# Spectral mixing and gated FFN: batch 0's first-stage results stored in thirds, and pieces moved in pairs

## The chip, the cores and the metric

One core of a Trainium2 chip runs one program. The metric is device time in microseconds (us); before the change it was 1681.91 us, the median of 3 runs (1680.63 to 1682.58). In the code `nc.tensor` is PE, `nc.vector` DVE, `nc.scalar` ACT, `nc.gpsimd` POOL, and `nc.sync` SP, the queue that issues every DMA of this kernel.

## The reference

```python
x: (8, 3136, 256)                     # w_in, conv_w, w_out are float64 on input
X = np.fft.rfft(x, axis=1)
Yr = Xr @ w_r - Xi @ w_i + b_r        # Yi likewise, with b_i
Y  = soft_threshold(Yr, 0.01), soft_threshold(Yi, 0.01)
y  = np.fft.irfft(Y, n=3136, axis=1)
h  = np.maximum(y @ w_in, 0)          # 256 -> 1024
c  = three-tap convolution of h along the sequence, per channel
out = (h * sigmoid(c)) @ w_out        # 1024 -> 256
```

Each batch goes through a transform along the sequence, a complex matrix product with bias and threshold, the inverse transform, and then a feed-forward layer with a gate. Nothing couples the batches.

## The kernel before, in words

The sequence of 3136 is 49 times 64. Each transform is done in two stages of matrix products, with tables made on the host.

**First stage (quads, L313).** A batch's x is cut into NX = 8 pieces. A piece holds 4 of 32 columns j for both halves h: 48 of the 49 rows n of half 0 on partitions 0 to 47, those of half 1 on 64 to 111, each partition with 4 KB that are contiguous in DRAM; row 48 goes to partitions 48 and 112 by a small DMA of its own. Eight passes of PE fill two PSUM banks; ACT (L330) and DVE (L331) copy one bank each into tile `a1`; `store_a1` writes 2 x 192 KB (and 8 KB of row 48) to DRAM scratch `sc1[b]`, in which unit g of the batch is 8 consecutive rows.

**Units.** A batch has NG = 6 units; two further ones hold the zero frequency of four batches each, so there are 50 iterations `it`. Iteration `it` runs, in PE's order: stage 3 of unit it-4 (L415), one or two pieces of a later batch (`quads`, by the table `count`), stage 2 of unit `it` (L359), and the complex product of unit it-1 (`mix`, L387, 36 matmuls). Stage 2 reads tile `a2`, 512 KB loaded from `sc1[b]` (`load_a2`, L346), which spreads (position, part) over 128 partitions. Because the first stage yields its rows the other way round, a unit's load needs the stores of all eight pieces of its batch: `ask_a2` issues it only when all of them are stored in program order, and on SP the load then waits until they have landed. `a2` has 3 buffers. Behind stage 2, ACT, DVE and POOL split values in two (`fh`, `fl`; the third pair by `third`, L370 on ACT and L371 on POOL), threshold (`shrink`, L403 to L405), and add the bias (`v`, L390). Stage 3's result goes to scratch `sc2` (L430).

**Head.** Batch 0 has no earlier batch to hide behind. Its x goes to tile `hx`, its results to `ha`; the loop at L485 copies a piece, stores it and asks for a further piece of x. NW = 9 times four passes on no new data (`ps_idle`) follow on PE. Then come the mixing weights (L214), the loads of units 0 and 1, one piece of batch 1's x, row 48's store (L499) and the bias, spread over 128 partitions by the DMA itself (L227). The pools `wkf`, `wk`, `cab`, `io` then take over the memory of `hx` and `ha`.

**Order and waits.** The whole front is in an order written by hand (`manual_schedule`). SP issues its DMAs one by one; as built they take eight completion semaphores in turn, so an issue waits for the landing of the DMA eight places ahead of it: at most eight are under way, whatever their size. Tables `t2` (second stage; POOL makes their lower half, L208) and `i1` (third stage) come in small loads during the first iterations. `fetch` keeps up to XRB = 4 pieces of x loaded; `a1` has 4 buffers.

**Last stages.** From about 472 us on, the feed-forward layer runs for all batches (L602, L630), fed by the last transform stage (L156).

Of the kernel before, what the change touches and what calls it, by code (L numbers as in the profile page):

```python
# [9 lines left out]
F32 = mybir.dt.float32  # L10
# [7 lines left out]
B, S, D, FF = 8, 3136, 256, 1024  # L18
R = 49
C = 64  # L20
U = (R - 1) // 2
# [4 lines left out]
UG = 4  # L26
# [83 lines left out]
def spectral_ffn_kernel(ctx: ExitStack, tc: tile.TileContext, x, w_r, w_i, b_r, b_i,  # L110
# [6 lines left out]
    sc1 = [dram.tile([RU, C, D], F32, name=f"sc1_{b}") for b in range(B)]  # L117
# [53 lines left out]
    with ExitStack() as ab:  # L171
# [13 lines left out]
        sgn = c0.tile([P, 2, C], F32, name="sgn")  # L185
        t2 = c1.tile([K2, U + 1, K2], F32, name="t2")
        bias = cmx.tile([P, 2, D], F32, name="bias")
        cmx.tile([P, 96], F32, name="pad")
# [10 lines left out]
            nc.sync.dma_start(f1, fwd1)  # L199

        def load_t2(g):
            sl = slice(g * UG, min((g + 1) * UG, U + 1))
            nc.sync.dma_start(t2[0:C, sl, :], fwd2v[:, sl, :])

        def fill_t2(g):
# [16 lines left out]
                split(wmix_hi[:, :, k, :], wmix_lo[:, :, k, :], w)  # L222

        def load_bias():

            for k in range(2):
                nc.sync.dma_start(bias[:, k, :], (b_r, b_i)[k].partition_broadcast(P))  # L227

        def load_inv1(g):
            if g < NG:  # L230
                sl = slice(g * UG // 2, (g + 1) * UG // 2)
# [72 lines left out]
        def load_x(pool, b, jc, **kw):  # L304

            xr = pool.tile([P, JC, D], F32, name="xr", **kw)
            xv = x[b].rearrange("(n h j) d -> h n j d", h=2, j=H)[:, :, jc * JC:(jc + 1) * JC, :]
            for h in range(2):
                nc.sync.dma_start(xr[SP * h:SP * h + RU], xv[h, 0:RU])
            nc.sync.dma_start(xr[RU:P:SP], xv[:, RU])  # L310
            return xr

        def quads(ps, xr):  # L313
# [3 lines left out]
                    rows = slice(SP * h, SP * h + R)  # L317
                    nc.tensor.matmul(ps[h][SP * r:SP * (r + 1)], f1[rows], xr[rows, 2 * r:2 * r + 2, :], start=True, stop=True)  # L318

        def store_a1(b, jc, a1, all_rows=True):  # L320
            dst = sc1[b].rearrange("m (c r j) d -> r c m (j d)", r=2, j=4)
            for r in range(2):
                nc.sync.dma_start(dst[r, jc], a1[SP * r:SP * r + RU].rearrange("p j h d -> p (j h d)"))  # L323
            if not all_rows:
                return
            dst = sc0[b // BH][b % BH].rearrange("(c r j) d -> c r (j d)", r=2, j=4)
            nc.sync.dma_start(dst[jc], a1[RU:P:SP].rearrange("p j h d -> p (j h d)"))

        def copy_a1(a1, ps):
            nc.scalar.copy(a1[:, :, 0], ps[0])  # L330
# [4 lines left out]
            quads(ps, xr)  # L335
            return ps

        def stage1_out(b, jc, ps):
            a1 = s1p.tile([P, 2, 2, D], F32, name="a1", bufs=4)
            copy_a1(a1, ps)  # L340
            store_a1(b, jc, a1)

        def load_a2(b, g):
            a2 = a2p.tile([K2, UG, D], F32, name="a2")
            if g < NG:
                nc.sync.dma_start(a2, sc1[b].rearrange("(u c) j d -> (c j) u d", c=2)[:, g * UG:(g + 1) * UG, :])  # L346
# [87 lines left out]

        nc.vector.memset(mlam, -LAM)
        nc.vector.memset(warm, 0.0)
        for q in range(4):
            nc.vector.memset(sgc[32 * q:32 * (q + 1)], -1.0 if q % 2 else 1.0)
        for c in range(2):
# [8 lines left out]
        xs, vs, ss, a2s, xq = {}, {}, {}, {}, []  # L448
        p1 = nx = NX

        def fetch(n):
            nonlocal nx
            while len(xq) < n and nx < n_pc:
                xq.append(load_x(s1p, *divmod(nx, NX), bufs=XRB))
                nx += 1

        def ask_a2(*its):
            for i in its:
# [5 lines left out]
        ab.enter_context(tc.manual_schedule())  # L464
        load_f1()
        with tc.tile_pool(name="hx", bufs=1, reuse_waits="tile") as hx, tc.tile_pool(name="ha", bufs=1, reuse_waits="tile") as ha:
            xh = hx.tile([P, H, D], F32, name="hx")
            ah = ha.tile([P, NX, 2, 2, D], F32, name="ha")
            xv = x[0].rearrange("(n h j) d -> h n j d", h=2, j=H)
            hr = sc0[0][0].rearrange("(c r j) d -> r c (j d)", r=2, j=4)  # L470
            asked = 0

            def ask_x():
                nonlocal asked
                if asked < NX:
                    if asked % 2 == 0:
                        sl = slice(asked * JC, (asked + 2) * JC)
                        nc.sync.dma_start(xh[RU:P:SP, sl], xv[:, RU, sl])
                    sl = slice(asked * JC, (asked + 1) * JC)
                    for h in range(2):  # L480
                        nc.sync.dma_start(xh[SP * h:SP * h + RU, sl], xv[h, 0:RU, sl])
                    asked += 1
            for _ in range(5):
                ask_x()
            for jc in range(NX):  # L485
                copy_a1(ah[:, jc], stage1_pe(xh[:, jc * JC:(jc + 1) * JC]))
                store_a1(0, jc, ah[:, jc], False)
                ask_x()
                if jc in (4, 5):
                    load_t2(jc - 4)  # L490
                    fill_t2(jc - 4)
            idle = [psx.tile([P, 2, D], F32, name="ps_idle", tag="bank") for _ in range(2)]
            for _ in range(NW):
                quads(idle, xh[:, (NX - 1) * JC:])
# [29 lines left out]

        for it in range(n_it + LAG):
            drain = it >= n_it
            fetch(XRB)
            if 1 < it + 2 < NG:
# [4 lines left out]
            if 0 <= it - 2 < NG:  # L533
# [10 lines left out]
            ps1 = [stage1_pe(xq.pop(0)) for _ in range(n_s1)] if it > 1 else []  # L544
            if it >= LAG:
                stage3_out(*g3, ps3)
            if WP0 <= it < Y0:
                next(background, None)
            elif it == WP0 - 2:
                next(background)  # L550
            for ps in ps1:
                stage1_out(*divmod(p1, NX), ps)
                p1 += 1
            ask_a2(it + 1)
            if WP0 <= it < Y0:
                for _ in range(2):
                    next(background, None)
            if it < n_it:
                xs[it] = stage2(items[it][1], a2s.pop(it))
            if it == Y0:  # L560
                eb.close()
                zio, y_a = pool("zio", 3, side="right"), pool("y_a", side="right")
                y0 = new_y(y_a)
                z2s = []
                for _ in range(3):
                    ask_z2()
            if it == n_it - 1:
                xs[it] = third(xs[it])
            if 0 <= it - 2 < n_it:
                ss[it - 2] = (clip if drain else shrink)(vs.pop(it - 2))  # L570
            if it < n_it - 1:
                xs[it] = third(xs[it])
            if Y0 < it < Y1:
                last_stage()
            if it == 1:
                stage1_out(*divmod(p1, NX), stage1_pe(xq.pop(0)))
                p1 += 1
# [113 lines left out]
```

## Time and profile before

| what | value |
|---|---|
| median of 3 runs | 1681.91 us |
| the profiled execution | 1683.23 us, of which its span 1681.5 us |
| PE busy | 1659.8 us (99%) |
| DVE, ACT busy | 1390.0 us, 1175.9 us |
| chain that ended last, by engine | PE 95%, DMA 3% |
| DMA | 162.50 MB, mean 97 GB/s; 235 to 282 GB/s in the first nine of 40 slices (to 378 us) |

The profile is one execution. The chain that ended last is followed back from the end: at each step to what released it. A row of the timeline has start, duration, engine, line, operation, tiles written and read, count, and in brackets the idle time before it with its releaser; a row named SPq is the issue of a DMA, not its transfer. A row of the waits has engine and line, what was waited for, the total, how many times, and the longest. A row of the windows has a stretch, and for each engine its busy time in it; its last three figures are PE's granted clock, the mean busy share of the 16 DMA engines, and the rate in GB/s.

### The profile page before, as it was taken

Reading aid. Unit: us, or ns where it says so; the run is one execution under the profiler, and the core shown is the slowest. Engines: PE = TensorE matmul, PEld = TensorE weight load, DVE = VectorE, ACT = ScalarE, POOL = GpSimd, SP = SyncE. Lnnn points to the kernel's source line nnn. Section 1 sums busy time; section 2 is a strip of 40 time slices with the busy share of each in tenths; the row PEclk is TensorE's granted clock in tenths of the full one; section 3 lists DMA queues with packets and bytes.
Section 4 is the critical chain, followed back from the end, with each engine's and each line's share of the span. In section 5 each row is a group of like instructions: output and inputs, shape, how many; then the busy total and the mean of one; then the engine's idle time right before and its main releaser. Section 6 shows DMA issues by size and latency. Waiting matters only on the chain.

```text
span 1681.5 us, 30439 instructions
## 1 busy us (share of the span) xinstructions
PE 1659.8 (99%) x12400; PEld 1539.7 (92%) x12400; DVE 1390.0 (83%) x1727; ACT 1175.9 (70%) x1584; POOL 192.3 (11%) x114
## 2 busy tenths in 40 slices
PE   7999999999999999999999999999999999999998
PEld 4778888889989999999999999999999999999998
DVE  2668988877688888888888888888888888888887
ACT  2667777777677777677777776777777776776776
POOL 1534444444300000000000000000000000000000
PEclk8999999999999999999999999999999999999999
DMA  8889999886421101111111001111101111100001
GB/s 240 241 282 277 280 269 269 265 235 186 116 71 51 51 33 42 51 51 42 50 35 41 33 30 50 42 51 51 33 32 51 47 38 51 42 23 23 23 23 44
DMA packets 110348, 162.50 MB, mean 97 GB/s; under 512 B 12136, under 2 KB 89610, under 8 KB 110202
## 3 DMA queue, kind: packets, MB, share of 16 engines
q1 hardware_dynamic: 110210, 160.57, 31.6%
q8 instruction: 98, 1.61, 0.4%
q14 instruction: 40, 0.33, 0.1%
HBM read 83.46 MB, written 77.07 MB: 95 GB/s over the span
## 4 chain that ended last, share of the span: by engine, by line
PE 95%; DMA 3%; issue 0%; DVE 0%; ACT 0%; SPq 0%; POOL 0%; ACTq 0%; POOLq 0%; DVEq 0%
PE ps_h L602 33%; PE acc L630 33%; PE ps_mx L387 12%; PE ps_s L156 7%; PE ps_s L359 5%; PE ps_s L318 3%; PE ps_s L415 3%; DMA a<-sc 1%; DMA hx<-in_x_dram 1%; DMA xr<-in_x_dram 1%; POOL fl L371 0%; DMA sc<-a 0%; PE ps_s L418 0%; DMA sc<-ha 0%; SPq L323 0%
## 5 line engine op out<-in xcount | busy, mean ns | idle before, releaser
L611 DVE SCALAR_TENSOR_TENSOR c<-h,cw,c 128x896 f32<-128x896 f32 x448 | 513.1, 1147 | 67.4 <-ACT c L609 66.1
L630 PE MATMUL acc<-wout,gh 128*128 128x256 f32 x3136 | 567.6, 281 | 0.4 <-ACT gh L616 0.4
L602 PE MATMUL ps_h<-yh,win 128*128 128x450 f32 x1792 | 549.1, 367 | 0.0
L630 PEld LDWEIGHTS acc<-wout,gh 128*128 128x128 f32 x3136 | 491.1, 188 | 6.4 <-ACT gh L616 0.6
L630 PE MATMUL acc<-wout,gl 128*128 128x256 f32 x1568 | 435.6, 280 | 0.0
L604 ACT ACTIVATE h<-ps_h 128x900 f32<-128x900 f32 x224 | 207.2, 925 | 234.3 <-PE ps_h L602 234.3
L602 PEld LDWEIGHTS ps_h<-yh,win 128*128 128x128 f32 x1792 | 338.7, 189 | 26.0 <-issue 0.4
L602 PE MATMUL ps_h<-yl,win 128*128 128x450 f32 x896 | 329.5, 368 | 0.0
L630 PEld LDWEIGHTS acc<-wout,gl 128*128 128x128 f32 x1568 | 293.2, 188 | 0.2
L613 DVE TENSOR_TENSOR c<-h,c 128x896 f32<-128x896 f32 x224 | 243.6, 1088 | 47.5 <-ACT c L612 46.9
L617 DVE TENSOR_TENSOR gl<-c,gh 128x896 fp32r<-128x896 f32 x224 | 243.1, 1088 | 34.4 <-ACT gh L616 30.3
L616 ACT CAST gh<-c 128x896 fp32r<-128x896 f32 x224 | 210.5, 944 | 77.1 <-DVE c L613 77.1
L612 ACT ACTIVATE c<-c 128x896 f32<-128x896 f32 x224 | 213.4, 953 | 28.4 <-DVE c L611 25.9
L602 PEld LDWEIGHTS ps_h<-yl,win 128*128 128x128 f32 x896 | 169.0, 189 | 11.3
L609 ACT ACTIVATE c<-h,cw 128x896 f32<-128x896 f32 x168 | 175.5, 1045 | 2.9 <-DVE gl L617 0.2
L387 PE MATMUL ps_mx<-wmix_hi,fh 128*128 128x256 f32 x600 | 172.4, 287 | 0.0
L387 PE MATMUL ps_mx<-wmix_hi,fl 128*128 128x256 f32 x600 | 167.6, 279 | 0.3 <-POOL fl L371 0.2
L387 PE MATMUL ps_mx<-wmix_lo,fh 128*128 128x256 f32 x600 | 167.7, 280 | 0.0
L405 POOL TENSOR_TENSOR r<-r,v 128x1024 f32<-128x1024 f32 x48 | 114.4, 2384 | 218.9 <-ACT v L404 209.0
L359 PEld LDWEIGHTS ps_s<-t,a 128*128 128x128 f32 (+1 forms) x800 | 96.0, 196 | 45.9 <-issue 30.6
L156 PEld LDWEIGHTS ps_s<-i,z 98*128 98x128 f32 x1024 | 122.4, 192 | 2.0 <-issue 0.8
L156 PE MATMUL ps_s<-i,z 98*128 98x98 f32 x1024 | 123.3, 273 | 0.0
(87 smaller groups left out, 1657.0 us busy)
## 6 DMA issues: line engine op xcount, KB each, us to landing
z<-sc SPq DMA_DIRECT2D x64, 392.0 KB
a<-sc SPq DMA_DIRECT2D x48, 512.0 KB
sc<-z SPq DMA_DIRECT2D x96, 256.0 KB
out_dram<-o SPq DMA_DIRECT2D x27, 896.0 KB
xr<-in_x_dram SPq DMA_DIRECT2D x112, 192.0 KB
sc<-a SPq DMA_DIRECT2D x112, 192.0 KB
hx<-in_x_dram SPq DMA_DIRECT2D x16, 192.0 KB
sc<-ha SPq DMA_DIRECT2D x16, 192.0 KB
```

The lines of the kernel that those rows point to most:

```text
L156: nc.tensor.matmul(to, z2[:, j, t * P:(t + 1) * P], i2[:, 0 if jg or j else 1, :], start=(j == 0), stop=(j == JG - 1), skip_group_check=True)
L359: nc.tensor.matmul(ps[:, k], a2[0:kk, k, t * P:(t + 1) * P], t2[0:kk, q, :], start=(k == 0), stop=(k == UG - 1), skip_group_check=True)
L387: nc.tensor.matmul(ps[c][:, k, :], lt, rh, start=(n == 0), stop=(n == len(mm) - 1))
L602: nc.tensor.matmul(ps[:, a, 0:CH + 2], lt, rh, start=(n == 0), stop=(n == len(mm) - 1))
L604: nc.scalar.activation(h, ps[:, :, 0:CH + 2], AF.Relu)
L609: nc.scalar.mul(c, h[:, :, 0:CH], cw[:, 0, f:f + 1])
L611: nc.vector.scalar_tensor_tensor(c, h[:, :, k:k + CH], cw[:, k, f:f + 1], c, op0=ALU.mult, op1=ALU.add)
L612: nc.scalar.activation(c, c, AF.Sigmoid)
L613: nc.vector.tensor_tensor(c, h[:, :, 1:CH + 1], c, op=ALU.mult)
L616: nc.scalar.copy(gh, c)
L617: nc.vector.tensor_tensor(gl, c, gh.bitcast(F32), op=ALU.subtract)
L630: nc.tensor.matmul(acc[m // 2][:, m % 2, :], lt[:, sl], rh[:, f, :], start=(f == 0 and n == 0 and m % 2 == 0), stop=(f == NF - 1 and n == ...
```

## The change

In six parts:
- **Pairs.** Pieces q and q+4 of a batch are loaded by one pair of DMAs (2 x 384 KB, row 48 with 16 KB) and stored by one (`put_x`, `store_a1`, `store_row`); the store is issued behind the second piece. XRB is now 3 pairs, `a1` has 2 buffers of a pair. `fetch` asks for one pair in an iteration. The tables `t2` and `i1` come for two units at a time.
- **Thirds.** Batch 0's results go to `sch[0..2]`, 16 of 48 rows (two units) each. In the head all of x is asked for first; the stores of the first third follow, a pair at a time; the second and third third are stored as a whole (2 x 512 KB each, from 16 partitions each) behind the loads of units 0 and 1.
- **Bias.** Two rows of 1 KB are loaded, and PE spreads them with a matmul against ones; ACT copies the result.
- **Row 48** of batch 0 is stored behind the last third.
- **Counts.** Iterations 1 to 4 take two pieces each, then 1, 2, 1, 1, 2, 1 in turn; batch 1 is complete in iteration 4, before in iteration 5. In iteration 1 the pieces stay between stage 2 and `mix`, and are now two.
- **NW** is 8 (was 9).

```diff
+    sch = [dram.tile([RU // 3, C, D], F32, name=f"sch_{k}") for k in range(3)]
...
-        DB, XRB = 1, 4
+        DB, XRB = 1, 3
...
-                nc.sync.dma_start(bias[:, k, :], (b_r, b_i)[k].partition_broadcast(P))
+                nc.sync.dma_start(brow[0:1, k], (b_r, b_i)[k].rearrange("(o e) -> o e", o=1))
+        def spread_bias():
+            ps = psx.tile([P, 2, D], F32, name="ps_b", tag="bank")
+            nc.tensor.matmul(ps, ones[0:1], brow[0:1], start=True, stop=True)
+            nc.scalar.copy(bias, ps)
...
+        def put_x(xr, b, q, ts=slice(0, 2)):
+            xv = x[b].rearrange("(n h t q j) d -> h n t q j d", h=2, t=2, j=JC, q=NX // 2)
+            for h in range(2):
+                nc.sync.dma_start(xr[SP * h:SP * h + RU, ts], xv[h, 0:RU, ts, q])
...
+        def store_third(k, cs, a1):
+            n = RU // 3
+            dst = sch[k].rearrange("m (c r j) d -> r m c (j d)", r=2, j=4)
+            for r in range(2):
+                nc.sync.dma_start(dst[r, :, cs], a1[SP * r + n * k:SP * r + n * (k + 1), cs].rearrange("p c j h d -> p c (j h d)"))
...
-            a1 = s1p.tile([P, 2, 2, D], F32, name="a1", bufs=4)
-            copy_a1(a1, ps)
-            store_a1(b, jc, a1)
+            if p % 2 == 0:
+                pair.append(s1p.tile([P, 2, 2, 2, D], F32, name="a1", bufs=2))
+            copy_a1(pair[-1][:, p % 2], ps)
+            if p % 2:
+                store_a1(b, c // 2, pair[-1])
+                store_row(b, slice(c // 2, NX, NX // 2), pair[-1])
...
-        LAG, WP0, LATE, NW = 4, 8, 10, 9
-        count = {1: 1, 2: 2, 3: 2, 4: 2, 5: 1, 6: 2, 7: 1, 8: 2, 9: 1, 10: 2}
+        LAG, WP0, LATE, NW = 4, 8, 10, 8
...
-            for jc in range(NX):
-                copy_a1(ah[:, jc], stage1_pe(xh[:, jc * JC:(jc + 1) * JC]))
-                store_a1(0, jc, ah[:, jc], False)
-                ask_x()
+            for i in range(NX):
+                q, t = divmod(i, 2)
+                c = t * (NX // 2) + q
+                copy_a1(ah[:, c], stage1_pe(xh[:, q, t]))
+                if i >= NX - 2:
+                    store_third(0, slice(c, c + 1), ah)
+                elif t:
+                    store_third(0, slice(q, NX, NX // 2), ah)
+            spread_bias()
...
             raw = load_mix()
             ask_a2(0, 1)
             fetch(1)
             split_mix(raw)
-            nc.sync.dma_start(hr, ah[RU:P:SP].rearrange("p c j h d -> p c (j h d)"))
-            load_bias()
+            store_third(1, slice(0, NX), ah)
+            fetch(1)
+            load_t2(2)
+            ask_a2(2)
+            store_third(2, slice(0, NX), ah)
+            store_row(0, slice(0, NX), ah)
...
-            n_s1 = min(count.get(it, (2, 1, 1, 2, 1, 1)[it % 6]) if it else 0, n_pc - p1)
+            n_s1 = min(2 if 0 < it < 5 else (1, 2, 1, 1, 2, 1)[(it - 5) % 6] if it else 0, n_pc - p1)
```

SP at the end of the head, before: the last stores of batch 0 (to `sc_0_59`) with a table between them, the weights, the loads of units 0 and 1, and batch 1's first piece.

```order
L323 DMA sc_0_59<-ha 48x1024 x4
L203 DMA t_118<-in_fwd_dram 64x512
L323 DMA sc_0_59<-ha 48x1024 x2
L203 DMA t_118<-in_fwd_dram 64x512
L323 DMA sc_0_59<-ha 48x1024 x4
L214 DMA wm_raw_289<-in_w_r_dram 128x2x256
L214 DMA wm_raw_290<-in_w_i_dram 128x2x256
L346 DMA a_293<-sc_0_59 128x4x256
L346 DMA a_295<-sc_0_59 128x4x256
L309 DMA xr<-in_x_dram 48x1024 x2
```

The same place now: x ends ahead of every store, `sch_66` is the first third and `sch_67`, `sch_68` the others, and unit 2's load (`a_311`) waits for the second third only.

```order
L314 DMA hx<-in_x_dram 48x2x1024 x2
L206 DMA t_122<-in_fwd_dram 64x1024
L345 DMA sch_66<-ha 32x1x1024 x6
L345 DMA sch_66<-ha 16x1024 x4
L369 DMA a_286<-sch_66 128x4x256
L369 DMA a_288<-sch_66 128x4x256
L314 DMA xr<-in_x_dram 48x2x1024 x2
L345 DMA sch_67<-ha 128x1x1024 x2
L206 DMA t_122<-in_fwd_dram 64x1024
L369 DMA a_311<-sch_67 128x4x256
L345 DMA sch_68<-ha 128x1x1024 x2
L314 DMA xr<-in_x_dram 48x2x1024 x2
```

Two thirds of batch 0's stores have moved behind the loads of units 0 and 1, the second between batch 1's first pairs of x, the last behind the load of unit 2. (Rows that only repeat are left out.)

SP around the first load of batch 1, before (`a_823` is unit 6, `a_817` the last piece of batch 1):

```order
L323 DMA sc_1_60<-a_711 48x1024 x2
L309 DMA xr<-in_x_dram 48x1024 x2
L232 DMA i_329<-in_inv_dram 128x128
L430 DMA sc_0_67<-z_813 64x1024 x2
L323 DMA sc_1_60<-a_817 48x1024 x2
L327 DMA sc_0_57<-a_817 2x1024
L346 DMA a_823<-sc_1_60 128x4x256
```

And now (`a_685` is the last pair of batch 1, `a_769` and `a_771` units 6 and 7):

```order
L453 DMA sc_0_69<-z_681 64x1024 x2
L335 DMA sc_1_59<-a_685 96x1x1024 x2
L339 DMA sc_0_57<-a_685 2x2x1024
L314 DMA xr<-in_x_dram 48x2x1024 x2
L317 DMA xr<-in_x_dram 2x2x1024
L369 DMA a_769<-sc_1_59 128x4x256
L369 DMA a_771<-sc_1_59 128x4x256
```

The last store of batch 1 stands behind the first store of stage 3 results, where before it stood behind the second; a pair of x lies between it and unit 6's load, which is asked for an iteration earlier.

More of the change, by code (lines that the diff above doesn't have):

```diff
@@ L116, in spectral_ffn_kernel @@
     sc0 = [dram.tile([BH, C, D], F32, name=f"sc0_{h}") for h in range(B // BH)]
-    sc1 = [dram.tile([RU, C, D], F32, name=f"sc1_{b}") for b in range(B)]
+    sc1 = [dram.tile([RU, C, D], F32, name=f"sc1_{b}") for b in range(1, B)]
+    sch = [dram.tile([RU // 3, C, D], F32, name=f"sch_{k}") for k in range(3)]
     sc2 = [dram.tile([C, R, D], F32, name=f"sc2_{b}") for b in range(B)]
@@ L185, in spectral_ffn_kernel @@
         sgn = c0.tile([P, 2, C], F32, name="sgn")
+        ones = c0.tile([P, P], F32, name="ones")
+        brow = c0.tile([P, 2, D], F32, name="brow")
         t2 = c1.tile([K2, U + 1, K2], F32, name="t2")
@@ L201, in load_t2 @@
         def load_t2(g):
-            sl = slice(g * UG, min((g + 1) * UG, U + 1))
+            sl = slice(g * UG, min((g + 2) * UG, U + 1))
             nc.sync.dma_start(t2[0:C, sl, :], fwd2v[:, sl, :])
@@ L318, in quads, with store_a1, store_row @@
                     nc.tensor.matmul(ps[h][SP * r:SP * (r + 1)], f1[rows], xr[rows, 2 * r:2 * r + 2, :], start=True, stop=True)
-        def store_a1(b, jc, a1, all_rows=True):
-            dst = sc1[b].rearrange("m (c r j) d -> r c m (j d)", r=2, j=4)
+        def store_a1(b, q, a1):
+            dst = sc1[b - 1].rearrange("m (t q r j) d -> r q m t (j d)", t=2, r=2, j=4, q=NX // 2)
             for r in range(2):
[L323 to L327, printed above, removed]
+                nc.sync.dma_start(dst[r, q], a1[SP * r:SP * r + RU].rearrange("p t j h d -> p t (j h d)"))
+        def store_row(b, cs, a1):
+            dst = sc0[b // BH][b % BH].rearrange("(c r j) d -> r c (j d)", r=2, j=4)
+            nc.sync.dma_start(dst[:, cs], a1[RU:P:SP].rearrange("p c j h d -> p c (j h d)"))
+        def store_third(k, cs, a1):
[3 more added lines that the diff above has]
+                nc.sync.dma_start(dst[r, :, cs], a1[SP * r + n * k:SP * r + n * (k + 1), cs].rearrange("p c j h d -> p c (j h d)"))
         def copy_a1(a1, ps):
@@ L345, in load_a2 @@
             if g < NG:
-                nc.sync.dma_start(a2, sc1[b].rearrange("(u c) j d -> (c j) u d", c=2)[:, g * UG:(g + 1) * UG, :])
+                src, u = (sc1[b - 1], g * UG) if b else (sch[g // 2], g % 2 * UG)
+                nc.sync.dma_start(a2, src.rearrange("(u c) j d -> (c j) u d", c=2)[:, u:u + UG, :])
             else:
@@ L436, in spectral_ffn_kernel @@
         nc.vector.memset(warm, 0.0)
+        nc.vector.memset(ones, 1.0)
         for q in range(4):
@@ L445, in spectral_ffn_kernel @@
         n_it, n_pc = len(items), B * NX
-        LAG, WP0, LATE, NW = 4, 8, 10, 9
-        count = {1: 1, 2: 2, 3: 2, 4: 2, 5: 1, 6: 2, 7: 1, 8: 2, 9: 1, 10: 2}
-        xs, vs, ss, a2s, xq = {}, {}, {}, {}, []
+        LAG, WP0, LATE, NW = 4, 8, 10, 8
+        xs, vs, ss, a2s, xq, pair = {}, {}, {}, {}, {}, []
         p1 = nx = NX
@@ L452, in fetch, with next_s1 @@
             nonlocal nx
-            while len(xq) < n and nx < n_pc:
-                xq.append(load_x(s1p, *divmod(nx, NX), bufs=XRB))
-                nx += 1
+            for _ in range(n):
+                if nx < min(n_pc, p1 // 2 * 2 + 2 * XRB):
+                    b, c = divmod(nx, NX)
+                    xq[nx // 2] = load_x(b, c // 2)
+                    nx += 2
+        def next_s1(p):
+            return stage1_pe(xq[p // 2][:, p % 2])
         def ask_a2(*its):
@@ L466, in spectral_ffn_kernel @@
         with tc.tile_pool(name="hx", bufs=1, reuse_waits="tile") as hx, tc.tile_pool(name="ha", bufs=1, reuse_waits="tile") as ha:
-            xh = hx.tile([P, H, D], F32, name="hx")
+            xh = hx.tile([P, NX // 2, 2, JC, D], F32, name="hx")
             ah = ha.tile([P, NX, 2, 2, D], F32, name="ha")
[L469 to L483, printed above, removed]
-                ask_x()
-            for jc in range(NX):
-                copy_a1(ah[:, jc], stage1_pe(xh[:, jc * JC:(jc + 1) * JC]))
-                store_a1(0, jc, ah[:, jc], False)
[L488 to L491, printed above, removed]
+            put_row(xh[:, 0], 0, 0)
+            for t in range(2):
+                put_x(xh[:, 0], 0, 0, slice(t, t + 1))
+            for q in range(1, NX // 2):
+                put_row(xh[:, q], 0, q)
+                put_x(xh[:, q], 0, q)
+            load_t2(0)
+            fill_t2(0)
+            fill_t2(1)
+            load_bias()
+            for i in range(NX):
[7 more added lines that the diff above has]
+            spread_bias()
             idle = [psx.tile([P, 2, D], F32, name="ps_idle", tag="bank") for _ in range(2)]
             for _ in range(NW):
-                quads(idle, xh[:, (NX - 1) * JC:])
+                quads(idle, xh[:, NX // 2 - 1, 1])
             raw = load_mix()
@@ L526, in spectral_ffn_kernel @@
             drain = it >= n_it
-            fetch(XRB)
-            if 1 < it + 2 < NG:
+            if it:
+                fetch(1)
+            if 2 < it + 2 < NG and it % 2 == 0:
                 load_t2(it + 2)
@@ L532, in spectral_ffn_kernel @@
                 load_inv1(NG)
-            if 0 <= it - 2 < NG:
+            if 0 <= it - 2 < NG and it % 2 == 0:
                 load_inv1(it - 2)
@@ L542, in spectral_ffn_kernel @@
                 ps3 = stage3_pe(g3[1], ss.pop(it - LAG))
-            n_s1 = min(count.get(it, (2, 1, 1, 2, 1, 1)[it % 6]) if it else 0, n_pc - p1)
-            ps1 = [stage1_pe(xq.pop(0)) for _ in range(n_s1)] if it > 1 else []
+            n_s1 = min(2 if 0 < it < 5 else (1, 2, 1, 1, 2, 1)[(it - 5) % 6] if it else 0, n_pc - p1)
+            ps1 = [next_s1(p1 + i) for i in range(n_s1)] if it > 1 else []
             if it >= LAG:
@@ L551, in spectral_ffn_kernel @@
             for ps in ps1:
-                stage1_out(*divmod(p1, NX), ps)
+                stage1_out(p1, ps)
                 p1 += 1
@@ L575, in spectral_ffn_kernel @@
             if it == 1:
-                stage1_out(*divmod(p1, NX), stage1_pe(xq.pop(0)))
-                p1 += 1
+                for _ in range(n_s1):
+                    stage1_out(p1, next_s1(p1))
+                    p1 += 1
             if 0 <= it - 3 < NG:
```

16 lines of the change are left out of this document (9 added, 7 removed).

## The prediction

> **What bounds the kernel now.** I read the page's busy times first, then PE's waits over the whole span, then the two places where they fall, as timeline and chain, and last the rate of the DMA rings by windows.
>
> ```profile
> span 1681.5 us, 30439 instructions
> PE 1659.8 (99%) x12400; PEld 1539.7 (92%) x12400; DVE 1390.0 (83%) x1727; ACT 1175.9 (70%) x1584; POOL 192.3 (11%) x114
> DMA  8889999886421101111111001111101111100001
> ```
>
> ```profile
> PE ps_s L359 <- DMA a<-sc: 9.9, 3, 5.3
> PE ps_s L318 <- DMA hx<-in_x_dram: 6.5, 3, 5.2
> PE acc L630 <- ACT gh L616: 0.4, 1, 0.4
> PE ps_mx L387 <- POOL fl L371: 0.2, 1, 0.2
> PE ps_s L318 <- ACT ha L330: 0.2, 1, 0.2
> ```
>
> PE is the bound, and waits 17.2 us in all: for batch 0's x, and for the loads of three units. The change neither adds nor takes PE work, but for one matmul and eight passes of `ps_idle`, so only these waits, the idle passes and PE's slow clock can be had. All but the 0.4 us of line 630 lie ahead of 91 us. The head's rows:
>
> ```profile
> 19.21 2.44 PE L318 MATMUL ps_s<-hx,f 49*64 49x512 f32 x8 [0.19 <-ACT ha L330]
> 20.95 9.33 PE L318 MATMUL ps_idle<-hx,f 49*64 49x512 f32 x72
> 21.69 0.69 DVE L331 COPY ha<-ps_s 128x512 f32<-128x512 f32 x1 [1.94 <-PE ps_s L318]
> 27.53 0.92 SPq L346 DMA_DIRECT2D a<-sc  x2
> 34.14 5.17 PE L359 MATMUL ps_s<-t,a 128*128 128x128 f32 x32 [3.86 <-DMA a<-sc]
> ```
>
> The last piece of x reaches PE at 19.21, its last copy ends at 22.38, the loads of units 0 and 1 are issued at 27.53, and the first useful product comes at 34.14. Stores and landings make the 5.15 us between copy and load:
>
> ```profile
> 24.41 3.04 DMA sc<-ha
> ...
> 79.21 3.60 DMA sc<-a
> 82.81 0.02 SPq L346
> 82.83 0.03 issue
> 82.86 4.23 DMA a<-sc
> 87.09 0.14 issue
> 87.23 3.75 PE ps_s L359 x16
> 90.99 4.54 PE ps_mx L387 x36
> 95.53 1.04 PE ps_s L415 x16
> 96.57 0.86 PE ps_s L318 x8
> 97.43 1.98 PE ps_s L359 x16
> 99.41 4.21 PE ps_mx L387 x36
> ```
>
> This is also the second place: unit 6, batch 1's first, waits for a store (3.60) and a load (4.23) one after the other, though its last piece had been copied long before. SP was late with that store:
>
> ```profile
> 73.14 0.59 ACT L330 COPY a<-ps_s 128x512 f32<-128x512 f32 x1
> ...
> 78.48 1.72 SPq L323 DMA_DIRECT2D sc<-a  x2
> ```
>
> Copied at 73.73, stored from 78.48: SP came to it only after earlier issues, each held by the DMA eight places ahead. Then PE restarts at half clock: 3.75 for 1.98, and 4.54 for 4.21, so 2.1 us beside the wait. The rates, the last figure of each row:
>
> ```profile
> 8.00:10.00 2.00, 2.00 (x13) 0.81 (x8) 0.83 (x2) 0.58 (x1) 0.00 (x0) 1.00 1.07 250
> 12.00:14.00 2.00, 1.70 (x10) 0.45 (x8) 0.93 (x2) 0.59 (x1) 0.00 (x0) 1.00 1.03 367
> 34.00:36.00 2.00, 1.86 (x9) 1.89 (x10) 0.69 (x1) 0.33 (x1) 0.00 (x0) 0.50 0.95 219
> 60.00:80.00 20.00, 20.00 (x195) 16.90 (x197) 13.47 (x24) 14.90 (x24) 10.44 (x7) 1.00 0.90 251
> 90.00:98.00 8.00, 8.00 (x70) 6.86 (x70) 5.11 (x9) 5.46 (x9) 3.63 (x2) 0.90 0.98 352
> 120.00:160.00 40.00, 40.00 (x380) 33.22 (x378) 34.36 (x58) 29.46 (x48) 19.01 (x10) 1.00 0.92 284
> 442.00:443.00 1.00, 1.00 (x12) 1.00 (x11) 1.00 (x3) 1.00 (x3) 0.00 (x0) 1.00 1.09 217
> ```
>
> Loads of x alone run at 250 GB/s with the engines full (1.07), loads and stores mixed at 367; ahead of the stall it is 251, later 284 to 352. At 442 one store from 64 partitions runs by itself: 217.
>
> **The change part by part.** I follow one instant, the start of unit 6's stage 2 (87.23 now). Behind it PE has no wait but 0.4 us of the 17.2, and the same work; so the new time is the old one plus this instant's shift, less what PE has done more by then, less clock saved.
>
> *Head.* Without stores between, x's 3.2 MB run at 250 rather than 367, but no longer share the ring: 12.8 us behind a start near 2.5, and 1.5 to 2 us more until PE has it, as in the rows of the head: 17.3 (19.21 now). Both pieces of the last pair come together: a second piece lies behind, 0.86 us at full clock and twice that at half; with the old way from x to copy (3.17) the last copy ends near 21.3 (22.38 now). Only two stores of 64 KB stand behind it; two issues at some 0.45 (the row of 27.53 has two in 0.92) and a landing of 3.04 give 25.2 for the loads (27.53 now; bounds 24, and 27.5 if the narrow stores of the first third are slow). I take 2.4 us off; from load to first product I keep 6.61, so PE starts at 31.7. NW takes 8 of 72 passes off (about 1 us of idle work); the idle passes end near 29, so PE rests under the 3.86 us after which it now starts at half clock (0.50 at 34).
>
> *Bias.* One matmul and one ACT copy (0.6 us, as the copy at 21.69) lie where PE and ACT wait for the loads; without that cover they would cost about 1.7 us. Two spread loads of 128 KB leave the ring: 1 us of it at 251, counted below. The `ones` memset is done before x comes; POOL's two table fills (L208) only move ahead, into its idle time.
>
> *Pairs.* Two pieces now take three places of the eight instead of six, so twice the bytes are under way. In the stretch from PE's start to unit 6 SP's order holds: weights 0.5 MB, seven unit loads 3.7, seven pairs of x 5.6, two thirds 2.1, row 48 0.1, four pair stores of batch 1 3.2, tables 0.8, one store of stage 3 results 0.5: 16.5 MB from about 24.5 on. At 251 GB/s that ends at 90.2, at 284 at 82.6, at 352 at 71.4. I take 284, the row of a long mixed stretch, since what held it at 251 was the number of places. The batch's last store is no longer last in line: a pair of x (0.8 MB, 2.8 us) lies between it and the unit's load and covers its landing.
>
> *Thirds.* Unit 2 needs the second third and units 4 and 5 the last, and each of them is read from 16 partitions at a time. Nothing in the trace is so narrow. Not slower than all: 284; the 64-partition store ran at 217; in proportion to partitions it would be 54. I take 217, the nearest row, since the 48-partition loads ran at 250, above it, so that the count alone does not rule: 2.1 MB cost 9.7 us instead of 7.4, 2.3 more. Unit 6: 84.9.
>
> *A new wait.* The tiles `r` and `v` lie where `ha` lay, so `shrink` of unit 0 (ACT) and the bias add of unit 1 (DVE) in iteration 2 wait for the last third's stores; behind them on ACT queue `third` of unit 2 and the next pair's copies. The last third lands some 5 us behind unit 2's load by this count, while PE is in `mix` (4.2) and waits for the next pair anyway: I take 0. With two `a1` buffers, pair 3's copies also wait for pair 1's store, which stands right behind a unit's load: 0 to 1, I take 0.4: 85.3.
>
> *PE's own chain* to unit 6 is 6 x 1.98 + 5 x 4.21 + 3 x 1.04 + 11 x 0.86 = 45.5 us from 31.7: 77.2. So the ring decides by 8 us, spread over iterations 1, 2, 3 and 6.
>
> *Sum.* 87.23 - 85.3 = 1.9 earlier; one piece more is behind PE by then (11 against 10), 0.9; the waits are several and mostly under 3.86, so most of the 2.1 us of slow clock goes: 1.9. In all 4.7 off the profiled 1683.23: 1678.5. That execution lay 1.3 above the median of 1681.91, so 1677.2.
>
> The Trainium skill speaks against the thirds (SBUF — State Buffer, Door 1: The DMA port swizzle): partitions 0 to 15 reach 4 of 16 DMA ports and 0 to 63 reach 8, at about 109 and 218 GB/s. The row at 442 agrees for 64 partitions (217); no row here shows 16. By the page's 109 the two thirds would cost 19.3 us and the sum would be that of the third rival.
>
> **The rivals.** A difference under 0.2% (3.4 us) can't be told from none here.
>
> *The ring runs free* (chance 0.20). With twice the bytes under way it holds the 352 of the row at 90, and the thirds cost no more than others. Then unit 6's data are there at 71.4, and PE's chain decides: 77.2 and about 2.5 of waits for pairs of x queued behind unit loads, 79.7. That is 7.5 earlier, with 0.9 and 2.1: 1671.4. For it: of the mixed stretches quoted, those with the engines full are at 352 and 367. Against it: the order now bunches loads of x, which alone hold 250.
>
> *No faster ring* (0.17). It stays at 251 because the unit loads wait for landings whatever the number of places. Unit 6 at 90.2, 3.0 later, less 0.9; the slow clock stays: 1684.0, no change to tell.
>
> *The thirds are slow* (0.15). If a store from 16 partitions gets half of what 64 get, 109 GB/s, two thirds hold the ring for 19.3 us instead of 7.4; loads behind them on the same rings wait, and the new waits of `shrink` and the bias add become long. Unit 6 at 82.6 + 11.9 = 94.5, 7.3 later, less 0.9, the slow clock as before: 1688.3. It decides as soon as unit 6 is later than 91.5, that is thirds under 128 GB/s.
>
> *Given back later* (0.06): the head gains, but a later batch's first unit, which waits for nothing now, waits again for its last pair. Against it, batch 2's first load is issued 7.2 us ahead of its use, and its last two pieces were stored together before too:
>
> ```profile
> 133.15 1.60 SPq L346 DMA_DIRECT2D a<-sc  x2
> ...
> 140.38 1.83 PE L359 MATMUL ps_s<-t,a 128*128 128x128 f32 x14
> ```
>
> Then about 1681.
>
> **How the numbers follow.** The forecast's case has 0.42: unit 6 between 82.5 and 86.5, 1674.5 to 1679. Predicted is 1677.2. The range runs from 1671, the free ring, to 1686, past the ring that is no faster, and leaves out most of the slow thirds (0.13) and a little below. Faster: 0.36 of the forecast's case and the free ring, 0.56. Same: 0.06 of the forecast's case, 0.17, 0.06 and 0.01 of the slow thirds, 0.30. Slower: 0.14.
>
> **What would show it.** Right: the first product (L359's line) near 31.7; unit 6's near 85 with no single wait of 5 us ahead of it; 280 or more GB/s between 40 and 80. The head is wrong if the loads of units 0 and 1 are issued after 27; the thirds if `mix` of unit 1 starts later than 50 (49.87 now) with SP waiting for `sch`; the later stretch if PE waits behind 100 us for a unit's load. The whole forecast is wrong if unit 6 starts behind 88, or if PE's work behind it takes another time than now.

## The result, and the profile after

The changed kernel takes 1693.72 us, the median of 4 runs (1693.21 to 1693.83); the kernel before 1682.01 (4 runs, 1680.63 to 1682.58). The ratio is 1.007, with an interval of 1.0053 to 1.0088: slower, where faster was forecast, and outside the range. The profiled execution took 1693.21 us. Every instant and rate below is from one execution of each kernel. The times of one kernel's executions differ by up to 7.4 us below (pairs of neighbours), so small differences between two profiles decide nothing.

The page's busy row of the changed kernel:

```profile
PE 1671.3 (99%) x12394; PEld 1538.5 (91%) x12394; DVE 1389.7 (82%) x1728; ACT 1176.6 (70%) x1585; POOL 192.4 (11%) x114
```

PE's waits over the whole span (engine and line, what was waited for, total, times, longest):

```profile
PE ps_s L330 <- DMA hx<-in_x_dram: 6.4, 4, 5.1
PE ps_s L382 <- DMA a<-sc: 4.8, 1, 4.8
PE ps_s L330 <- DMA xr<-in_x_dram: 2.0, 1, 2.0
PE ps_mx L410 <- DVE fl L388: 1.9, 1, 1.9
PE acc L660 <- ACT gh L646: 0.4, 1, 0.4
```

The waits are fewer (15.5 us against 17.2), and yet the kernel is slower. "Busy" PE hides the rest: part of the 1671.3 us is idle passes and passes at half clock. So I follow instants, not sums. The timeline of the changed kernel, PE and SP's issues:

```profile
28.22 10.27 PE L330 MATMUL ps_idle<-hx,f 49*64 49x512 f32 x64
38.42 3.84 PE L382 MATMUL ps_s<-t,a 128*128 128x128 f32 x32
29.63 0.92 SPq L369 DMA_DIRECT2D a<-sch  x2
```

The loads of units 0 and 1 are issued at 29.63 (27.53 before; 25.2 forecast), the first product comes at 38.42 (34.14 before; 31.7 forecast). The chain at unit 6:

```profile
83.57 7.31 DMA sc<-a
...
90.96 6.40 DMA a<-sc
...
97.49 3.75 PE ps_s L382 x16
101.24 5.02 PE ps_mx L410 x36
...
108.16 1.98 PE ps_s L382 x16
110.14 4.20 PE ps_mx L410 x36
```

Unit 6 starts at 97.49 (87.23 before; 85.3 forecast), behind a store and a load as before, and again at half clock: 3.75 for 1.98 and 5.02 for 4.20. It is 10.26 later; one piece more is behind PE by then (0.9), and the slow clock costs 2.6 instead of 2.1: 9.9 us in all, of the 10.0 between the two profiled executions. So the whole loss lies ahead of unit 6, in two stretches: 2.1 us up to the loads of units 0 and 1, and 67.9 us from there to unit 6 where the kernel before took 59.7. The rates by windows (last three figures: granted clock, DMA share, GB/s):

```profile
8.00:10.00 2.00, 1.94 (x9) 0.26 (x4) 0.70 (x2) 0.59 (x1) 0.00 (x0) 1.00 1.02 168
12.00:14.00 2.00, 1.74 (x10) 0.46 (x10) 0.00 (x0) 0.59 (x1) 0.00 (x0) 1.00 1.07 164
60.00:80.00 20.00, 19.46 (x139) 14.82 (x140) 9.40 (x17) 11.11 (x20) 9.67 (x8) 0.83 1.03 265
```

In the head the DMA engines are as full as before (1.02 and 1.07) and move 168 and 164 GB/s, not 250 and 367.

### The profile page after: what moved, and what is told of

Read it like the earlier page. It is cut to its first block, busy times and chain, and to the rows that moved or that the text cites. A ratio compares the mean times of both kernels' runs of the same rounds, so it can differ in the third digit from the quotient of the medians.

```text
span 1691.2 us, 30084 instructions
## 1 busy us (share of the span) xinstructions
PE 1671.3 (99%) x12394; PEld 1538.5 (91%) x12394; DVE 1389.7 (82%) x1728; ACT 1176.6 (70%) x1585; POOL 192.4 (11%) x114
## 4 chain that ended last, share of the span: by engine, by line
PE 93%; DMA 2%; issue 1%; DVE 0%; POOL 0%; ACT 0%; SPq 0%; ACTq 0%; POOLq 0%; DVEq 0%
PE ps_h L632 33%; PE acc L660 33%; PE ps_mx L410 11%; PE ps_s L157 7%; PE ps_s L382 5%; PE ps_s L438 3%; PE ps_s L330 2%; DMA sc<-a 2%; DMA a<-sc 0%; POOL fl L394 0%; PE ps_s L441 0%; DVE fl L388 0%; DVE v L415 0%; ACT o L666 0%; POOL t L211 0%
```

## The experiments

Four theories after the result. **H**, the order of halves: a load of 384 KB keeps all DMA engines on one half of the partitions for too long, and the halves run one after the other. **F**: pieces q and q+4 are read more slowly than neighbours. **T**: the narrow stores of the thirds hold the ring (the DMA engines and what is queued on them). **I**: the idle passes, which end at 38.42, set the start. Each run is read by the two instants above, from its own timeline: the issue of the loads of units 0 and 1, and unit 6's stage 2.

**Single loads.**

```diff
-            for h in range(2):
-                nc.sync.dma_start(xr[SP * h:SP * h + RU, ts], xv[h, 0:RU, ts, q])
+            for t in range(ts.start, ts.stop):
+                for h in range(2):
+                    nc.sync.dma_start(xr[SP * h:SP * h + RU, t], xv[h, 0:RU, t, q])
```

> The changed kernel, but each load of a pair of x issued as two loads of 192 KB, in the order h0, h1 of the first piece, then h0, h1 of the second; stores, counts and tiles as in it. Theory H (order of halves: a 384 KB load keeps all DMA engines on one half of the partitions for too long, so that the two halves run one after the other at some 165 GB/s, while small loads in turn overlap at 245): batch 0's x is in by 18.5 (22.5 in the changed kernel), the first product comes at 34 to 36 (38.4), 768 KB of a later pair land in 3.3 us (4.6), unit 6 near 89 (97.5), 1684 to 1686 us. Theory F (far pieces: pieces q and q+4, 16 KB apart in DRAM, are read more slowly than neighbours, in whatever lengths): nothing changes by more than 1 us, 1692 to 1694. Theory T (the narrow stores of the thirds hold the ring) and theory I (the idle passes end too late): the same 1692 to 1694, though under T the x of batch 0 may well come earlier.

Measured: 1687.72 us (6 runs, ratio to before 1.0036, 1.0024 to 1.0047). Its timeline:

```profile
24.64 0.92 SPq L370 DMA_DIRECT2D a<-sch  x2
32.42 0.38 PE L383 MATMUL ps_s<-t,a 128*128 128x128 f32 x1
91.11 0.46 PE L383 MATMUL ps_s<-t,a 128*128 128x128 f32 x2 [3.81 <-DMA a<-sc]
```

The loads go out 5.0 us earlier and the first product comes 6.0 us earlier; that is the head as it was forecast (25.2 and 31.7). From the issue to unit 6 it is still 66.5 us. So the length of the loads costs the head 5 us and the later stretch next to nothing (67.9 and 66.5). The windows of this run show the head's rate back:

```profile
8.00:10.00 2.00, 2.00 (x15) 0.73 (x12) 0.85 (x2) 0.58 (x1) 0.00 (x0) 1.00 1.04 248
12.00:14.00 2.00, 2.00 (x12) 0.64 (x8) 0.98 (x2) 0.59 (x1) 0.00 (x0) 1.00 1.02 234
```

**Pairs of neighbours.**

```diff
-            xv = x[b].rearrange("(n h t q j) d -> h n t q j d", h=2, t=2, j=JC, q=NX // 2)
+            xv = x[b].rearrange("(n h q t j) d -> h n t q j d", h=2, t=2, j=JC, q=NX // 2)
...
```

> The changed kernel, but a pair is pieces 2q and 2q+1, neighbours in DRAM (8 KB in a row), instead of q and q+4; loads of 384 KB as in it. Theory H: no change, x in at 22.5, unit 6 at 97, 1692 to 1694. Theory F: x in by 18.5, 768 KB of a later pair in 3.3 us, unit 6 near 89, 1684 to 1686. Theories T and I: 1692 to 1694.

Measured: 1693.77 us (4 runs), as the changed kernel. Three of the four took 1693.55 to 1694.40; the profiled one took 1686.97, with the loads issued at 27.95 and unit 6 at 93.96, at full clock behind a wait of 3.05. Even in it the head's windows (8 to 10 and 12 to 14) run at 193 and 176 GB/s, not at the 248 and 234 of single loads. F falls.

**Fewer idle passes.** NW = 2 instead of 8.

> The changed kernel with 2 rounds of idle passes instead of 8 (NW). Theory I: the idle passes ran past the landing of unit 0's data (34.95) and unit 1's (36.95) to 38.42, and that delay is handed on: first product at 35 to 37, unit 6 earlier by the same 1.5 to 3, 1690 to 1692. Theories H, F and T (the ring alone sets unit 6): first product at 35 to 37, unit 6 within 0.7 of 97.5, 1692.5 to 1694.

Measured: 1692.27 us (4 runs, ratio 1.0057, 1.0042 to 1.0072), between the two forecasts, so the instants must decide.

```profile
28.81 0.92 SPq L369 DMA_DIRECT2D a<-sch  x2
34.45 0.55 PE L382 MATMUL ps_s<-t,a 128*128 128x128 f32 x1 [3.35 <-DMA a<-sch]
97.13 0.55 PE L382 MATMUL ps_s<-t,a 128*128 128x128 f32 x1 [4.55 <-DMA a<-sc]
```

PE starts 4 us earlier, and unit 6 comes 0.4 us earlier: theory I falls. What unit 6 waits for is a DMA, and PE's earlier start did not bring that DMA forward.

**The shapes alone.** A kernel without any computation: six kinds of loading 3.1 MB of x to the partitions of the kernel, each waited for as a whole, all six a second time, then three kinds of storing as much. `pair_adj` takes pieces 2q and 2q+1, and `pair_two` has the loads of the second half issued by ACT.

```python
def pair_far(b):
    t = seg("pair_far")
    for q in range(Q):
        for h in range(2):
            nc.sync.dma_start(t[SP * h:SP * h + RU, q:NX:Q], view(b)[h, 0:RU, q:NX:Q])
    end(t)
```

> No kernel of the work: it only moves data and leaves all of the computation out. Each stretch loads 3.1 MB of x into 48 + 48 partitions and waits for all of it; then three stretches store as much. Theory H: one_adj (192 KB, neighbours, halves in turn) and one_far (192 KB, pieces q and q+4, halves in turn) at 240 to 250 GB/s, some 13 us each; pair_far and pair_adj (384 KB) at 160 to 175, 18 to 20 us; one_half (192 KB, all of one half first) as slow as these or slower; pair_two (384 KB, the halves from two engines' queues) back at 240. Theory F: one_adj, pair_adj and one_half at 245, and one_far, pair_far and pair_two at 165 to 200. Stores: by both theories w in single pieces and in pairs at 300 or more; by theory T the stores by 16 partitions at half of that or less.

Measured (one run), by windows inside each stretch, in this order: one_adj, pair_far, pair_adj, one_far, one_half, pair_two; stores singly, in pairs, by 16 partitions (three figures at the end: clock, DMA share, GB/s):

```profile
1.00:17.00 16.00, 0.00 (x0) 0.00 (x0) 1.00 0.96 196
20.00:34.00 14.00, 0.00 (x0) 0.00 (x0) 1.00 1.02 198
41.00:55.00 14.00, 0.00 (x0) 0.00 (x0) 1.00 1.02 171
60.00:72.00 12.00, 0.00 (x0) 0.00 (x0) 1.00 1.03 229
77.00:95.00 18.00, 0.16 (x1) 0.00 (x0) 1.00 1.03 154
100.00:111.00 11.00, 0.00 (x0) 0.00 (x0) 1.00 1.03 228
237.00:248.00 11.00, 0.00 (x0) 0.00 (x0) 1.00 0.86 265
251.00:263.00 12.00, 0.07 (x1) 0.00 (x0) 1.00 0.86 243
266.00:285.00 19.00, 0.07 (x1) 0.00 (x0) 1.00 0.88 150
```

The second time the six loads run at 195, 188, 179, 226, 158 and 227. H holds in kind: all of one half first is slowest (154 and 158), pairs are slower than the same pieces singly (198 against 229, 171 against 196, and in the second round too), and two queues bring pairs back to 228. But the loss is 8 to 17%, not the third expected. F is wrong the other way round: neighbours are the slower order here. And stores by 16 partitions run at 150, those by 48 at 265, a loss of 43%: T's price.

**Two queues in the head.** The loads of half 1 of batch 0 issued by ACT.

> The changed kernel, but in the head the loads of the second half of the partitions are issued by ACT, those of the first by SP; still 384 KB each. Theory H (the halves run one after the other in one queue): as with single loads, x in by 18.5 (22.5 in the changed kernel, 18.7 with single loads), the first product at 32 to 34.5, unit 6 at 91 to 93, 1686 to 1688. If the length of a load itself is slow, whatever the queue: x in at 22, first product at 38, 1692 to 1694.

Measured: 1693.97 us (4 runs), no gain; the loads of units 0 and 1 issued at 30.18, and the windows of the head at 191 and 174 GB/s. SP's timeline of this run:

```profile
1.96 0.82 SPq L314 DMA_DIRECT2D hx<-in_x_dram  x2
...
8.79 0.33 SPq L314 DMA_DIRECT2D hx<-in_x_dram  x1
```

The expectation failed. SP waits for places, 2.2 us with a small load of row 48 (L317) and 4.1 us with the loads themselves (L314), and half 0 goes out late (8.79 for its third pair), when ACT has issued the last load of half 1 at 4.63: the two halves were not offered side by side as they were in the kernel that only moves data. It does not speak against H, and does not support it.

**Whole stores.** Two further theories for the later stretch. **M**: in the head of the kernel before, stores ran beside loads and cost little; moved behind the unit loads they cost the ring their full time. **P**: the pairs slow the later stretch. Batch 0 is stored whole again, 48 rows of a pair at a time, with pair loads, and then with single loads too.

```diff
-                    store_third(0, slice(q, NX, NX // 2), ah)
+                    store_all(slice(q, NX, NX // 2), ah)
...
-            store_third(1, slice(0, NX), ah)
...
-            store_third(2, slice(0, NX), ah)
```

> The changed kernel with batch 0's results stored whole: all 48 rows of a pair right behind it (384 KB a half), no thirds; pairs of x, bias and counts as changed. Theory M (moved stores: in the kernel before, the stores of the head ran beside the loads of x, 367 GB/s in both directions together, and cost little; put behind the unit loads, the last two thirds cost the full 10.8 us that they take there): the first product at 38 to 41, but from it to unit 6's stage 2 only 50 to 54 us (59.1 in the changed kernel, 53.1 in the one before), unit 6 near 91, 1685 to 1688 us. Rival P (the pairs slow the later stretch, the thirds little): from the first product to unit 6 still 57 to 60 us, unit 6 at 96 or later, 1692 or more.

> Both undone: batch 0's results stored whole and each load of x split in two of 192 KB; bias, counts, pair stores of the later batches as changed. Theory M with the slow pairs of the head: the first product at 34 to 36, 50 to 54 us to unit 6, unit 6 at 85 to 89, 1680 to 1684 us, that is no difference from the kernel before that can be told. Rival P' (the pair stores, the counts or the two a1 buffers slow the later stretch): 57 us or more to unit 6, 1686 or more.

Measured: 1685.96 us with pair loads (10 runs, ratio 1.0022, 1.0013 to 1.0032), 1683.01 with single loads (10 runs, 1.0007, 0.9998 to 1.0016). The timelines, with pair loads and with single ones:

```profile
31.14 0.92 SPq L368 DMA_DIRECT2D a<-sch  x2
90.17 0.55 PE L381 MATMUL ps_s<-t,a 128*128 128x128 f32 x1 [4.84 <-DMA a<-sc]
```

```profile
31.51 0.92 SPq L369 DMA_DIRECT2D a<-sch  x2
90.47 0.35 PE L382 MATMUL ps_s<-t,a 128*128 128x128 f32 x1 [2.46 <-DMA a<-sc]
```

59.0 us from issue to unit 6 in both. From the first product, by which the expectations were put, it is 54.4 us with pair loads (35.80) and 51.8 with single ones (38.63): near M's 50 to 54, and not the 57 or more of P and P', which fall. It is the thirds that make 66.5 to 67.9 of the 59.0. The rates from 30 to 90 us, in the kernel before, the changed one, and these two runs:

```profile
30.00:90.00 60.00, 49.91 (x421) 41.06 (x418) 34.16 (x59) 33.76 (x59) 22.65 (x18) 0.93 0.85 240
30.00:90.00 60.00, 56.10 (x444) 41.01 (x440) 32.80 (x58) 31.93 (x55) 20.14 (x17) 0.94 0.99 254
30.00:90.00 60.00, 53.76 (x464) 39.85 (x456) 34.83 (x60) 33.55 (x58) 22.64 (x18) 0.99 1.03 250
30.00:90.00 60.00, 50.61 (x440) 39.65 (x432) 35.02 (x60) 34.00 (x58) 22.72 (x18) 0.94 0.92 247
```

Pair loads keep the engines fuller (1.03 against 0.92) and move hardly more (250 against 247 GB/s). M's later stretch is right, but the head pays: the loads go out at 31.14 and 31.51, later than in the kernel before (27.53) and, with single loads, 6.9 us later than with thirds. Both unit 6s come within 0.3 us of each other; the 2.6 us between the two profiled executions are the clock, which fell to half behind the wait of 4.84 and not behind 2.46.

**The thirds alone**, in the kernel before:

```diff
-                store_a1(0, jc, ah[:, jc], False)
+                store_third(0, slice(jc, jc + 1), ah)
...
+            store_third(1, slice(0, NX), ah)
+            fetch(2)
+            ask_a2(2)
+            store_third(2, slice(0, NX), ah)
```

> The kernel before with the thirds alone (batch 0's first third behind each piece, the second behind the loads of units 0 and 1, the third behind that of unit 2); single pieces, bias by spread loads, counts as before. Theory M: the head gains, the first product at 31 to 33 (34.1 in the kernel before), but the moved stores cost 58 to 61 us from there to unit 6 (53.1), unit 6 at 90 to 93 (87.2), 1684.5 to 1688. Rival P (the thirds pay, the pairs spoil it): 50 to 54 us, unit 6 at 82 to 86, 1677 to 1681.

Measured: 1695.25 us (4 runs, ratio 1.0074, 1.0057 to 1.0091), worse than M expected.

```profile
25.37 0.92 SPq L352 DMA_DIRECT2D a<-sch  x2
30.62 0.38 PE L365 MATMUL ps_s<-t,a 128*128 128x128 f32 x1
57.42 1.24 PE L319 MATMUL ps_s<-xr,f 49*64 49x512 f32 x4 [15.39 <-DMA xr<-in_x_dram]
100.45 0.55 PE L365 MATMUL ps_s<-t,a 128*128 128x128 f32 x1 [3.37 <-DMA a<-sc]
```

The head gains 3.5 us, as expected, and 75.1 us follow to unit 6. Here the next pieces of x stand on SP behind the thirds, row 48 and the bias, are issued from 50.83 only, and PE waits 15.39 us for one. So the thirds, in this place, lose without any pair.

**The rest in one part.** On the run with single loads, rows 16 to 47 stored from 32 partitions a half at once.

```diff
-    sch = [dram.tile([RU // 3, C, D], F32, name=f"sch_{k}") for k in range(3)]
+    sch = [dram.tile([n, C, D], F32, name=f"sch_{n}") for n in (RU // 3, 2 * RU // 3)]
...
-            store_third(2, slice(0, NX), ah)
```

> As the run with single loads (1687.72 us, 66.5 us from the issue of the loads of units 0 and 1 to unit 6's stage 2), but rows 16 to 47 of batch 0 stored as one part from 32 partitions a half, instead of two parts from 16; unit 2 then waits for all of it. Theory N (narrow stores are slow by themselves: 150 GB/s in the kernel that only moves data, single stores from 48 partitions 265): 2.1 MB in 8 to 9 us instead of 14, 62 to 64 us from issue to unit 6, 1683.5 to 1685.5. Theory M alone (what counts is that 2.1 MB were moved behind the unit loads, whatever their shape): 66 to 67 us, 1687 to 1688.5.

Measured: 1683.41 us (11 runs, ratio 1.0005, 0.9996 to 1.0014), 4.3 us under the run with single loads.

```profile
25.83 0.92 SPq L370 DMA_DIRECT2D a<-sch  x2
89.26 0.55 PE L383 MATMUL ps_s<-t,a 128*128 128x128 f32 x1 [5.40 <-DMA a<-sc]
```

63.4 us from issue to unit 6, as N says. The same bytes behind the loads of units 0 and 1, from twice the partitions, and 4.3 us less. The order is not quite the same: what was the last third now goes out ahead of unit 2's load and of a pair of x, where before it stood behind them. The narrow shape is the likelier cause, as the kernel that only moves data shows it slow by itself; the two were not separated. What is still moved (63.4 against 59.0) is given back by the earlier loads.

**In turn.** Whole stores and single loads, but in the head five pieces of x are asked for ahead, then one behind each store, as in the kernel before. The head's stores are single pieces again too.

```diff
+            for _ in range(5):
+                ask_x()
...
-                    store_all(slice(q, NX, NX // 2), ah)
+                store_all(slice(c, c + 1), ah)
+                ask_x()
```

> Batch 0 stored whole and x loaded singly, as in the run with both undone, but the head's loads and stores issued in turn as in the kernel before (five pieces ahead, then one load behind each store) instead of all loads first. If loads and stores of the head pay only when they run side by side: the loads of units 0 and 1 issued at 26 to 28 (31.5 in the run with both undone), 59 us from there to unit 6, unit 6 at 85 to 87, 1679 to 1681.5 us. If the order of issue in the head doesn't matter: as that run, 1682 to 1684.

**The last rows later.** On top of it, rows 16 to 47 of the last two pieces stored behind the loads of units 0 and 1.

> The run with loads and stores in turn, but of the last two pieces only rows 0 to 15 are stored ahead of the loads of units 0 and 1, rows 16 to 47 (0.5 MB, 32 partitions a half) behind them. By the sum of issue and ring: the loads 1.5 to 2.5 us earlier, 2 us more from there to unit 6 (0.5 MB at 250 GB/s), so unit 6 within 1 us of the run in turn, and the time within 1.5 us of it. If small stores ahead of the loads pay in themselves: unit 6 2 us earlier and 1677 to 1679.

Measured: 1678.06 us in turn (11 runs, ratio 0.9981, 0.9973 to 0.9990), and 1677.69 with the last rows later (11 runs, 0.9978, 0.9969 to 0.9987). The timeline in turn:

```profile
27.84 1.95 SPq L369 DMA_DIRECT2D a<-sch  x2
36.24 0.38 PE L382 MATMUL ps_s<-t,a 128*128 128x128 f32 x1
84.94 0.35 PE L382 MATMUL ps_s<-t,a 128*128 128x128 f32 x1 [0.67 <-DMA a<-sc]
```

The rates from 12 to 14 us, loads and stores in turn first, all loads first second:

```profile
12.00:14.00 2.00, 2.00 (x14) 0.91 (x12) 0.69 (x1) 0.59 (x1) 0.00 (x0) 1.00 1.05 348
12.00:14.00 2.00, 2.00 (x12) 0.45 (x9) 0.80 (x2) 0.59 (x1) 0.00 (x0) 1.00 1.07 238
```

With stores between the loads the engines, no fuller, move 348 GB/s and not 238. Against the run that loads all of x first, the loads of units 0 and 1 go out 3.7 us earlier and unit 6 starts 5.5 us earlier; its wait is down to 0.67; the time is a little under the 1679 to 1681.5 expected. Both versions beat the kernel before by some 0.2% and the changed one by 0.9%. Between the two there is no difference in time, as the sum said. In the profile of the second the loads go out 1.8 us earlier (26.01) and unit 6 comes 1.7 us later (86.65), but that execution took 1682.12, 4.4 us above its median, and so shows little of the others.

**Far pieces alone**, in the kernel before: its pieces in the order 0, 4, 1, 5, 2, 6, 3, 7.

> The kernel before, with its pieces taken in the order 0, 4, 1, 5, 2, 6, 3, 7 instead of 0 to 7; nothing else. In the kernel that only moves data single loads of this order ran at 229 GB/s, of neighbours in turn at 196. If that holds in the kernel: 5.6 MB of x take 2 to 4 us less of the ring between the loads of units 0 and 1 and unit 6, unit 6 at 83.5 to 85.5 (87.2), 1678 to 1680. If the order of pieces doesn't matter beside stores: 1681 to 1683.

Measured: 1681.91 us (11 runs, ratio 0.9999, 0.9990 to 1.0007). No effect on the time: the 229 against 196 GB/s of loads alone brings nothing in a ring that mixes them with stores and unit loads.

## Why the prediction was wrong

**That only the stretch ahead of unit 6 counts** was right: behind it there is no wait but 0.4 us, and 9.9 of the 10.0 us are found at that instant and in the clock.

**Head: failed.** "x's 3.2 MB run at 250" took the rate of single loads in turn from one half to the other for pairs. With pairs it was 168 and 164 in the same windows, the loads went out at 29.63 and not at 25.2. With single loads they went out at 24.64 and PE started at 32.42 (31.7 forecast): the rest of that step held. It cost 4.4 us against the forecast at the issue. Why pairs lose a third here, and 8 to 17% in the kernel that only moves data, stays open. The idle passes, forecast to end near 29, ended at 38.42, but that cost nothing at unit 6.

**Pairs: failed,** and this is the larger miss. "What held it at 251 was the number of places" is not so: 59.0 us from issue to unit 6 with pair loads, 59.0 with single loads, 59.7 in the kernel before. From 30 to 90, with twice the bytes under way, the engines' share rose from 0.85 to 0.99, but the rate only from 240 to 254: busier engines, not more moved. (The forecast's 284 was reached from 60 to 80 in the run with whole stores and pair loads, but not held over the stretch, 250.) Nor did the pair of x behind the batch's last store cover its landing: that store took 7.31 us and unit 6's load behind it 6.40, where the kernel before had 3.60 and 4.23. Of the forecast's 60.1 us for this stretch 9.7 were the thirds, so 50.4 stood for the rest, which took 59.0: 8.6 us.

**Thirds: the size was nearly right, and its place in the sum was not weighed.** They were priced at 9.7 us of the ring; the runs with and without them differ by 7.5 (single loads) and 8.9 (pair loads). That it came so near has luck in it: the rate taken was 217, and alone such stores run at 150. But I set against them only a head relieved of stores, and did not ask what the stores had cost there. With loads and stores in turn the loads of units 0 and 1 go out at 27.84 with all of batch 0 stored; thirds and single loads bring 24.64. So 3.2 us are gained for 7.5.

A rule of the Trainium skill (SBUF — State Buffer, Door 1: The DMA port swizzle) stood against the thirds: partitions 0 to 15 reach about 109 GB/s. The stores by 16 partitions, halves in turn, ran at 150 alone, between that and its 218 for 64 partitions. The rival that it stood beside decided under 128 GB/s, and so did not come in; the thirds cost what the forecast took for them.

**Bias** cost nothing that can be seen. **The new waits** were larger than taken: ACT's copies of the third pair waited 5.0 us for a store that still held their `a1` buffer, where 0.4 was taken, and `shrink` waited 1.9 us for the store of row 48, where 0 was taken. The first stands in the chain that led to unit 6; what it cost by itself no run shows. With whole stores and single loads it is gone. **The slow clock** was forecast to go (1.9) and stayed, 0.5 larger, because PE still meets unit 6 with one long wait (4.83). A wait under 3.86 is no safety either: in the run with two queues half clock came behind 3.30.

The sum: 4.4 of the head, 8.6 of the pairs, less 0.8 of the thirds, make unit 6 12.2 us later than forecast; with 2.4 of clock the forecast of 1678.5 for the profiled execution becomes 1693.1, and 1693.21 was measured. That the sum closes proves little, as its parts are differences of the same instants; the runs carry the causes. Of the rivals "no faster ring" was right about the ring. It kept the forecast's head, and that is 4.4 of the 7.3 us by which its unit 6 (90.2) came too early; its time came out 9.7 us too low.

What the runs price in times: the pair loads 6.0 us (1693.72 to 1687.72; 3.0 with whole stores, 1685.96 to 1683.01), the narrow stores, with their order, 4.3 (to 1683.41), and, with whole stores, loading all of x ahead of the stores and storing it by pairs 5.0 (1683.01 to 1678.06). What is then left of the change (bias by PE, counts, pair stores of the later batches, merged tables, the buffers, the later row 48, one round of idle passes less) beats the kernel before by 0.1 to 0.3%. Which of these parts does it was not tried.

## What to carry to other kernels

A rate belongs to a shape and an order, not to a queue: before a transfer is merged or moved, find a row with the same partitions, the same bytes in a row and the same neighbours in the queue, and do not take more bytes under way for more bytes moved. Before stores are moved out of a stretch, ask what they cost where they stand: beside loads it may be much less than elsewhere (here 3.2 us against 7.5). And follow instants (the issue of a load, the start of the work that needs it): the sum of waits fell here while the kernel became slower.

## What the runs showed of the hardware

- Loads to 48 of 64 partitions, without stores: 154 and 158 GB/s (first and second round) when one half comes first; when 192 KB to each half alternate, 196 and 195 for neighbours, 229 and 226 for far pieces; when 384 KB do, 171 and 179, 198 and 188. The Trainium skill (SBUF — State Buffer, "Can I just issue two DMAs to hit both halves?") says that two transfers at once, at partitions 0 and 64, gain 6%. Here alternating gained 23 to 49% for short loads and 11 to 29% for long ones, so the measurement decides. That the DMA engines' order between the halves is the cause is argued from these rates; the two-queue run in the kernel did not confirm it.
- Stores by 16 partitions a half, halves in turn: 150 GB/s; by 48: 265.
- At unit 6 PE came back at half clock (3.75 or 3.76 for 1.98) in eight executions that had waited 3.30 to 5.40 us there, took 3.37 behind 6.28 and 2.64 behind 3.81, and came back at full clock (2.02) behind 3.05, 2.46 and 0.67. In the changed kernel's trace the granted clock from 97.50 to 101.00 is 0.50. So the same instant is worth some 2 us more or less by the clock that PE gets there, and the length of the wait does not settle it alone.
